# Listing all engines' order in the second network of a linear-attention and two-network kernel, with sums in place and its second layer bank by bank

## The chip, the core and the metric

The kernel runs on one core of a Trainium2 chip. The core has five engines that run their own instruction lists in order: TensorE (PE, matrix products into PSUM), VectorE (DVE), ScalarE (ACT), GpSimd (POOL) and SyncE (SP), which here issues nearly all DMAs. The metric is the time of one execution on the device in microseconds, as the median of several runs.

## What is computed

```python
def reference(q, k, v, alpha, moe_w_in, moe_w_out, domain_probs, w1, w2):
    for t in range(768):                               # linear attention, 4 batches, 8 heads, 48 wide
        state = alpha[:, :, t, :, None] * state + einsum('bhd,bhe->bhde', k[:, :, t], v[:, :, t])
        y[:, :, t] = einsum('bhd,bhde->bhe', q[:, :, t], state)
    x = tokens(y)                                      # 3072 x 384
    x = elu(x @ w_in) @ w_out                          # first network, hidden 2048
    p = domain_probs / (domain_probs.sum(-1, keepdims=True) + 1e-9)
    for e in range(4):                                 # second network, 4 experts, hidden 1024 each
        out += p[:, e:e + 1] * (relu(x @ w1[e]) @ w2[e])
    return out
```

## The kernel before

All large products keep float32 accuracy by splitting every operand into a high part in the TensorE format `fp32r` and a remainder: `hi` by a cast, `low = value - hi` by a subtraction. One 128x128 by 128x512 product then is three matmuls (hi·hi, hi·low, low·hi).

The attention and the first network fill the first 546 us. The change touches the second network, at the end of `run`. Its tokens are worked on in three *pairs* r of 1024 tokens (two chunks of 512); a pair has two halves m of 512 columns and three 128-row blocks of the model's width. The hidden units of all four experts are 32 blocks of 128, taken three at a time: a *group* i = 11 r + q is three hidden blocks (two for q = 10), so there are 33 groups.

*Layer 1* of a group (`layer1`, L699) needs the product of a 3x3 weight block by a 3x2 x block, 18 tile products; a bilinear scheme does it with 15 (`STEPS`, 11 for q = 10: `STEPS2`). Each of the 15 steps multiplies one precomputed sum of weights by one precomputed sum of x tiles (three matmuls, L717) into one of two PSUM banks `h0` and `h1` in turn, and DVE adds the bank into running sums `u` (L731 to L737). Two of the additions per group run on POOL, `u<-u` in step 7 and `c<-u` in step 8, and one on DVE has both its inputs in SBUF, `u<-u` in step 7. Six steps (5, 8, 10, 12, 13 and 14) finish a hidden tile (m, f): (1,2), (1,0), (1,1), (0,2), (0,1), (0,0). A finished tile lies in a buffer `c`; `relu` (L693) has ACT write its `hi` (L695) and the ReLU in place (L696), and POOL the remainder into `g` (L697). The `c` buffers come from `ctile` (L640), five in rotation, out of pools that others share: every fifth lies in the tag `g` of the pool `hp`, three buffers, where the `xh` tiles below live too.

*Layer 2* of group i-1 (`layer2`, L745) runs on PE between the steps of layer 1 of group i: the list `work` is cut by a count of DVE operations (`cut`) and a piece is issued after each step. A group with three hidden blocks has 54 matmuls (two halves, three output blocks d, three hidden blocks f, three matmuls each) into six PSUM banks `oa[m, d]`, named a0, a1, h2 for m = 1 and t0, t1, t2 for m = 0. When an expert's last hidden block is done in a bank, `gate` (L776) has DVE multiply the bank by the expert's probability into a `c` (for the first expert straight into `acc`) and POOL add it to `acc` (L787). So an ordinary group is 45 + 54 = 99 matmuls. Gates fall in q = 3, 6, 8 and in q = 0 of the next pair, where SP then stores `acc` to the output.

*The next pair's x.* The 15 sums of x tiles for pair r + 1 are made during pair r by `prep_x` (L607): a load of the raw x and 15 times `one`, which adds up tiles on POOL (L633), casts `hi` on ACT and writes the remainder on POOL (`split`, L370), into a tile `xh` that SP stores to DRAM (L636). `load_xc` brings them back as `xc` when the old ones are free. Groups q = 1 to 7 take up to three of these 16 jobs each, after steps 1, 6 and 11.

*What sets the order.* In the first network the instructions of PE, ACT, DVE and POOL stand as the program writes them (`tc.manual_schedule`), and `later` puts a function in a queue that the next `flush` runs, so that a dependent instruction is listed some work behind the one it waits for. In the second network only PE is listed by hand; a scheduler orders ACT, DVE, POOL and SP from its own estimate, and `later` runs its function at once. Nothing orders SP by hand in either.

Of the kernel before, what the change touches and what calls it, by code (L numbers as in the profile page):

```python
# [86 lines left out]
class _Fast:  # L87
# [605 lines left out]
    def relu(self, g, n, v):  # L693
# [3 lines left out]
        nc.gpsimd.tensor_tensor(out=g[:, n, 1], in0=v, in1=g[:, n, 0].bitcast(F32), op=ALU.subtract)  # L697

    def layer1(self, i, extra):  # L699
# [45 lines left out]
    def layer2(self, i, G):  # L745
# [14 lines left out]
        if i == NPR * NG - 1:  # L760
            runs = [[(t, d) for t in items if t[0] == m] for m in (1, 0) for d in range(KD)]
        for run in runs:
            for (m, f), d in run:
                e, n = divmod(hid(f), F2)
                for j, (wl, gl) in enumerate(((0, 0), (0, 1), (1, 0))):
                    def mm(m=m, f=f, d=d, wl=wl, gl=gl, e=e, first=n == 0 and j == 0, last=n == F2 - 1 and j == 2):
                        nc.tensor.matmul(  # L767
                            oa[m, d], wt[:, f, wl, d * 128:(d + 1) * 128], G[m][:, f, gl], start=first, stop=last
                        )
                        if last:  # L770
                            self.gate(r, e, m, d)

                    l.append(mm)
# [424 lines left out]
```

## Time and profile before

| what | value |
|---|---|
| median of 3 runs | 1299.26 us (1299.12 to 1302.6) |
| the profiled execution | 1300.14 us, its span 1298.3 us |
| PE busy | 1249.2 us, 96% of the span |
| DVE busy | 896.5 us, 69% |
| ACT busy | 585.6 us, 45% |
| POOL busy | 521.5 us, 40%, nearly all of it in the second network |
| chain that ended last | PE 78%, DVE 9%, ACT 4%, POOL 3% of the span |

Matmuls are pipelined, so a busy PE is not a PE at its best rate; the distance from one matmul's start to the next's is the better measure, and the length of a group is taken from it. A profile's time stamps belong to one execution, the one of 1300.14 us. A wait is put down to the semaphore that came last.

### The profile page before, as it was taken

How to read it: one execution, taken by the hardware profiler on the slowest of the kernel's cores; microseconds unless marked ns; L12 is line 12 of the kernel's file. 1: busy time of each engine (PE TensorE's matmuls, PEld its weight loads, DVE VectorE, ACT ScalarE, POOL GpSimd, SP SyncE). 2: the span in 40 equal slices, each digit the busy share in tenths (PEclk: the TensorE clock that was granted, in tenths of full speed). 3: DMA queues.
4: the chain of work that ended last, by engine and by line, in shares of the span. 5: the costliest groups of instructions: out<-in, count | busy, mean ns of one | idle time of the engine just before them, and what ended most of it. 6: DMA issues, size and time to landing. Idle time of an engine off the chain costs nothing.

```text
span 1298.3 us, 17667 instructions
## 1 busy us (share of the span) xinstructions
PE 1249.2 (96%) x6457; PEld 1013.5 (78%) x6457; DVE 896.5 (69%) x1510; ACT 585.6 (45%) x1076; POOL 521.5 (40%) x405
## 2 busy tenths in 40 slices
PE   8887899999999999899999999899999999999997
PEld 6665788888888788778878887788878878888886
DVE  8988677786777757666757666566767576657664
ACT  5665556666666666544342323334332233233241
POOL 0000000000000005478776656887956465456562
PEclk8998999999999999999999999999999999999999
DMA  6554156564756455727646458755644574425232
GB/s 226 201 177 141 62 182 219 189 207 170 250 189 211 167 189 206 275 91 255 231 175 230 150 191 319 266 204 203 249 166 169 206 293 172 176 103 206 98 114 72
DMA packets 71535, 246.70 MB, mean 190 GB/s; under 512 B 6680, under 2 KB 38264, under 8 KB 62096
## 3 DMA queue, kind: packets, MB, share of 16 engines
q1 hardware_dynamic: 70576, 240.77, 52.4%
q10 hardware_dynamic: 864, 4.72, 0.9%
q8 instruction: 53, 0.87, 0.3%
q14 instruction: 42, 0.34, 0.1%
HBM read 182.11 MB, written 63.36 MB: 189 GB/s over the span
## 4 chain that ended last, share of the span: by engine, by line
PE 78%; DVE 9%; ACT 4%; POOL 3%; issue 3%; DMA 1%; SPq 0%; POOLq 0%; ACTq 0%; DVEq 0%
PE h L717 22%; PE t L767 13%; PE h L417 12%; PE t L445 12%; PE a L767 9%; PE h L767 4%; DVE u L737 1%; PE a L247 1%; PE a L304 1%; PE a L311 1%; DVE w_W L373 1%; DVE cv L79 1%; DVE cv L82 1%; DMA xraw<-x1d 1%; POOL g_W L697 1%
## 5 line engine op out<-in xcount | busy, mean ns | idle before, releaser
L737 DVE TENSOR_TENSOR u<-h,u 128x512 f32<-128x512 f32 x258 | 177.6, 688 | 91.0 <-PE h L717 89.8
L417 PE MATMUL h<-x,w_W 128*128 128x512 f32 x864 | 219.8, 398 | 11.6 <-DVE w_W L373 7.0
L717 PE MATMUL h<-xc_Q,wa 128*128 128x512 f32 x780 | 220.2, 392 | 5.0 <-DVE c L737 2.4
L445 PE MATMUL t<-g,w_W 128*128 128x512 f32 x864 | 214.8, 392 | 3.5 <-DVE g L435 3.5
L697 POOL TENSOR_TENSOR g_W<-c,g_W 128x512 fp32r<-128x512 f32 x128 | 164.4, 1300 | 125.9 <-ACT c L696 108.0
L562 POOL TENSOR_TENSOR xs<-xr 128x512 f32<-128x512 f32 x8 | 11.1, 1405 | 482.0 <-DMA xr<-x1d 482.0
L695 ACT ACTIVATE g_W<-c 128x512 fp32r<-128x512 f32 x128 | 80.0, 626 | 276.5 <-DVE c L737 163.9
L417 PEld LDWEIGHTS h<-x,w_W 128*128 128x128 f32 x864 | 161.4, 190 | 50.4 <-DVE w_W L373 10.4
L445 PEld LDWEIGHTS t<-g,w_W 128*128 128x128 f32 x864 | 160.7, 188 | 38.6 <-DVE g L435 4.7
L717 PEld LDWEIGHTS h<-xc_Q,wa 128*128 128x128 f32 x780 | 146.2, 188 | 38.5 <-DVE u L737 4.4
L767 PE MATMUL t<-g_W,wb 128*128 128x512 f32 x576 | 157.6, 389 | 0.0
L767 PEld LDWEIGHTS t<-g_W,wb 128*128 128x128 f32 x576 | 108.1, 188 | 22.6 <-POOL g_W L697 0.2
L696 ACT ACTIVATE c<-c 128x512 f32<-128x512 f32 x192 | 121.0, 632 | 7.7 <-ACT g_W L695 0.4
L737 DVE TENSOR_TENSOR c<-u,h 128x512 f32<-128x512 f32 x123 | 84.1, 686 | 51.7 <-PE h L717 37.9
L428 DVE SCALAR_TENSOR_TENSOR h<-e,h 128x512 f32<-128x512 f32 x96 | 66.5, 693 | 74.0 <-ACT e L427 74.0
L717 PE MATMUL h<-xc_W,wa 128*128 128x512 f32 x390 | 110.9, 393 | 6.1 <-DVE u L737 4.1
L731 DVE COPY u<-h 128x512 f32<-128x512 f32 x99 | 68.1, 691 | 68.1 <-PE h L717 67.8
L767 PE MATMUL a<-g_W,wb 128*128 128x512 f32 x384 | 113.6, 395 | 0.7 <-POOL g_W L697 0.7
L697 POOL TENSOR_TENSOR g_X<-c,g_X 128x512 fp32r<-128x512 f32 x64 | 82.2, 1296 | 62.5 <-ACT c L696 51.9
L695 ACT ACTIVATE g_X<-c 128x512 fp32r<-128x512 f32 x64 | 40.0, 627 | 142.5 <-DVE c L737 78.4
L435 DVE TENSOR_TENSOR g<-h,g 128x512 fp32r<-128x512 f32 x96 | 65.9, 686 | 41.1 <-ACT g L433 40.7
L717 PEld LDWEIGHTS h<-xc_W,wa 128*128 128x128 f32 x390 | 73.2, 189 | 23.9 <-DVE u L737 5.5
(138 smaller groups left out, 1948.6 us busy)
## 6 DMA issues: line engine op xcount, KB each, us to landing
wa<-wad SPq DMA_DIRECT2D x33, 1536.0 KB, 6.5
wb<-wbd SPq DMA_DIRECT2D x30, 1536.0 KB, 7.2
raw<-in_att_dram SPq DMA_DIRECT2D x22, 960.0 KB, 4.9
wad<-wh SPq DMA_DIRECT2D x44, 384.0 KB, 2.7
wbd<-wh SPq DMA_DIRECT2D x43, 384.0 KB, 3.5
xcd<-xh SPq DMA_DIRECT2D x30, 512.0 KB, 3.0
wraw<-in_wm_dram SPq DMA_DIRECT2D x16, 768.0 KB, 4.2
wraw<-in_we_dram SPq DMA_DIRECT2D x20, 576.0 KB, 4.5
```

The lines of the kernel that those rows point to most:

```text
L79: nc.vector.scalar_tensor_tensor(out=t, in0=top, scalar=-0x80000000, in1=t, op0=ALU.bitwise_and, op1=ALU.bitwise_or)
L417: nc.tensor.matmul(h[:, 0:n], w[:, wl, fi, k * 128:(k + 1) * 128], x[:, xl, k, n0:n0 + n], start=(k == 0 and i == 0), stop=(k == KD - 1 an ...
L428: nc.vector.scalar_tensor_tensor(out=h, in0=e, scalar=-1.0, in1=h, op0=ALU.add, op1=ALU.max)
L435: 0, lambda: nc.vector.tensor_tensor(out=g[:, 1], in0=h, in1=g[:, 0].bitcast(F32), op=ALU.subtract)
L445: nc.tensor.matmul(self.xa[k][:, 0:n], w[:, wl, fi, DM + k * 128:DM + (k + 1) * 128], g[:, gl, 0:n], start=(first and i == 0), stop=(last ...
L695: nc.scalar.activation(out=g[:, n, 0], in_=v, func=AF.Relu)
L696: nc.scalar.activation(out=v, in_=v, func=AF.Relu)
L697: nc.gpsimd.tensor_tensor(out=g[:, n, 1], in0=v, in1=g[:, n, 0].bitcast(F32), op=ALU.subtract)
L717: nc.tensor.matmul(b, w[:, wl], x[:, xl], start=(j == 0), stop=(j == 2))
L731: nc.vector.tensor_copy(out, b)
L737: (nc.vector if "b" in (a0, a1) or dst == "S5" else nc.gpsimd).tensor_tensor(out=out, in0=val(a0, b), in1=val(a1, b), op=ALU.add if op == ...
L767: nc.tensor.matmul(oa[m, d], wt[:, f, wl, d * 128:(d + 1) * 128], G[m][:, f, gl], start=first, stop=last)
```

## The change

1. The listed order of PE, ACT, DVE and POOL is kept on through the second network, and so is the queue: `layer1` flushes it at the start of each step. The remainder of a ReLU (`relu`) and the addition of a gate (`gate`) are put in the queue once, so they stand behind the next flush. `later` gets a count n, by which a function waits n flushes.
2. `one` adds its tiles up in the place of the remainder, `t[:, 1]`, and takes no `c`; the cast is listed two flushes later, remainder and store three. Two jobs per group, after steps 2 and 9, in q = 1 to 8. The load of the first `xc` tile moves from step 0 to step 4 of q = 9.
3. `layer2` sorts its products by expert, half, output block d, hidden block f, where before it was expert, half, f, d. The last group already stood bank by bank.

```diff
-    def later(self, f):
+    def later(self, f, n=1):
         if self.queue is None:
             f()
+        elif n > 1:
+            self.queue.append(lambda: self.later(f, n - 1))
         else:
             self.queue.append(f)
...
-            t = self.hp.tile([128, 2, 512], F32R, tag="g", name="xh")
+            t = self.hp.tile([128, 2, 512], F32, tag="g", name="xh")
             l = terms(p)
             v = x[l[0][0]]
-            if len(l) > 1:
-                c = self.ctile()
-                for u, sign in l[1:]:
-                    nc.gpsimd.tensor_tensor(out=c, in0=v, in1=x[u], op=ALU.add if sign > 0 else ALU.subtract)
-                    v = c
-            self.split(t[:, 0], t[:, 1], v, nc.gpsimd)
-            nc.sync.dma_start(out=self.xcd[r - 1][n // 3][:, n % 3], in_=t.bitcast(F32))
+            for u, sign in l[1:]:
+                nc.gpsimd.tensor_tensor(out=t[:, 1], in0=v, in1=x[u], op=ALU.add if sign > 0 else ALU.subtract)
+                v = t[:, 1]
+            hi = t[:, 0].bitcast(F32R)
+
+            def low():
+                nc.gpsimd.tensor_tensor(out=t[:, 1].bitcast(F32R), in0=v, in1=t[:, 0], op=ALU.subtract)
+                nc.sync.dma_start(out=self.xcd[r - 1][n // 3][:, n % 3], in_=t)
+
+            self.later(lambda: nc.scalar.copy(hi, v), 2)
+            self.later(low, 3)
...
-        nc.gpsimd.tensor_tensor(out=g[:, n, 1], in0=v, in1=g[:, n, 0].bitcast(F32), op=ALU.subtract)
+        self.later(
+            lambda: nc.gpsimd.tensor_tensor(out=g[:, n, 1], in0=v, in1=g[:, n, 0].bitcast(F32), op=ALU.subtract)
+        )
...
+            self.flush()
             b = self.hbank()
...
-        runs = [[(t, d)] for t in items for d in range(KD)]
+        items = sorted(((hid(f) // F2, -m, d, f) for m, f in items for d in range(KD)))
...
+        if r < NPR - 1 or e < NE - 1:
+            self.later(lambda: add(nc.gpsimd))
+        else:
+            add(nc.vector)
...
-        self.queue = None
-        order.__exit__(None, None, None)
...
-                if 1 <= q <= 7:
-                    for n, s in enumerate(xs[(q - 1) * 3:q * 3]):
-                        put(1 + 5 * n, do, s)
+                if 1 <= q <= 8:
+                    for n, s in enumerate(xs[(q - 1) * 2:q * 2]):
+                        put(2 + 7 * n, do, s)
```

Three places show what this does to the engines' lists. First POOL in group 12 (pair 1, q = 1), where the raw x of the next pair arrives. `g<-c,g` is a remainder, `u<-u` and `c<-u` are layer 1's two additions, `c<-xraw` and then `xh<-xraw` a sum. Before:

```order
L697 TENSOR_TENSOR g_W_7555<-c,g_W_7555 128x512
L737 TENSOR_TENSOR u<-u 128x512
L737 TENSOR_TENSOR c<-u 128x512
L633 TENSOR_TENSOR c<-xraw 128x512 x2
L697 TENSOR_TENSOR g_W_7555<-c,g_W_7555 128x512
L633 TENSOR_TENSOR c<-c,xraw 128x512 x2
L697 TENSOR_TENSOR g_W_7555<-c,g_W_7555 128x512
L373 TENSOR_TENSOR xh<-c,xh 128x512 x2
```

And POOL in the same group now:

```order
L704 TENSOR_TENSOR g_W_7541<-c,g_W_7541 128x512
L746 TENSOR_TENSOR u<-u 128x512
L746 TENSOR_TENSOR c<-u 128x512
L704 TENSOR_TENSOR g_W_7541<-c,g_W_7541 128x512
L633 TENSOR_TENSOR xh<-xraw 128x512
L633 TENSOR_TENSOR xh<-xh,xraw 128x512 x2
L704 TENSOR_TENSOR g_W_7541<-c,g_W_7541 128x512
L638 TENSOR_TENSOR xh<-xh 128x512
```

The sums of one product instead of two stand there, behind the remainder of tile (1,0) and ahead of that of (1,1), and they write no `c`.

Second, DVE in group 8 (pair 0, q = 8) from step 5 to step 10, where `c<-a,pb`, `c<-h,pb` and `c<-t,pb` are gates of the six banks and the others are layer 1. Before:

```order
L737 TENSOR_TENSOR c<-h_6843,u 128x512
L786 TENSOR_TENSOR c<-a_5441,pb 128x512
L737 TENSOR_TENSOR u<-h_6860,u 128x512
L786 TENSOR_TENSOR c<-a_5442,pb 128x512
L737 TENSOR_TENSOR u<-h_6871,u 128x512
L786 TENSOR_TENSOR c<-h_5443,pb 128x512
L737 TENSOR_TENSOR u<-u 128x512
L737 TENSOR_TENSOR u<-h_6886,u 128x512
L733 SCALAR_TENSOR_TENSOR u<-h_6899,u 128x512
L737 TENSOR_TENSOR c<-u,h_6907 128x512
```

And DVE over the same steps now:

```order
L746 TENSOR_TENSOR c<-h_6827,u 128x512
L792 TENSOR_TENSOR c<-a_5438,pb 128x512
L746 TENSOR_TENSOR u<-h_6844,u 128x512
L746 TENSOR_TENSOR u<-h_6852,u 128x512
L746 TENSOR_TENSOR u<-u 128x512
L792 TENSOR_TENSOR c<-h_5439,pb 128x512
L746 TENSOR_TENSOR u<-h_6867,u 128x512
L742 SCALAR_TENSOR_TENSOR u<-h_6880,u 128x512
L746 TENSOR_TENSOR c<-u,h_6890 128x512
L792 TENSOR_TENSOR c<-t_5434,pb 128x512
```

One gate now stands at step 2 (ahead of these rows), one at step 5, one after `u<-u` of step 7, and the next at step 10.

Third, PE at the start of a group without gates (group 2: pair 0, q = 2), where L717 is layer 1 and L767 layer 2 of the group before, banks a, a, h of the half m = 1. Before:

```order
L717 MATMUL h_5646<-xc_Q_4865,wa 128x512 x3
L767 MATMUL a_5441<-g_W_5511,wb 128x512 x2
L717 MATMUL h_5658<-xc_Q_4865,wa 128x512 x3
L767 MATMUL a_5441<-g_W_5511,wb 128x512
L767 MATMUL a_5442<-g_W_5511,wb 128x512 x3
L717 MATMUL h_5675<-xc_Q_4865,wa 128x512 x3
L767 MATMUL h_5443<-g_W_5511,wb 128x512 x3
L767 MATMUL a_5441<-g_W_5511,wb 128x512
```

And PE at the same place now:

```order
L726 MATMUL h_5636<-xc_Q_4865,wa 128x512 x3
L773 MATMUL a_5437<-g_W_5508,wb 128x512 x2
L726 MATMUL h_5648<-xc_Q_4865,wa 128x512 x3
L773 MATMUL a_5437<-g_W_5508,wb 128x512 x4
L726 MATMUL h_5659<-xc_Q_4865,wa 128x512 x3
L773 MATMUL a_5437<-g_W_5508,wb 128x512 x3
L773 MATMUL a_5438<-g_W_5508,wb 128x512
```

The first nine matmuls of layer 2 now go to one bank and read all three hidden tiles of the half; before, they read the first tile alone, three matmuls to each bank.

## Rows read from the trace of the kernel before

**Rows 1.** The page: engines' busy time; and one costly group, with its mean duration

```profile
PE 1249.2 (96%) x6457; PEld 1013.5 (78%) x6457; DVE 896.5 (69%) x1510; ACT 585.6 (45%) x1076; POOL 521.5 (40%) x405
...
L695 ACT ACTIVATE g_W<-c 128x512 fp32r<-128x512 f32 x128 | 80.0, 626 | 276.5 <-DVE c L737 163.9
```

**Rows 2.** PE's waits, 560 us to the end: total us, times, longest us

```profile
PE h L717 <- DVE u L737: 6.4, 7, 3.9
PE h L717 <- DVE c L737: 4.3, 4, 2.2
PE a L767 <- POOL g_W L697: 0.7, 1, 0.7
PE h L717 <- DVE ok L802: 0.4, 1, 0.4
```

**Rows 3.** Groups 1, 5, 7, 8, 11, 12, 13, 17, 23: start:end, length, PE, PEld, DVE, ACT, POOL, clock

```profile
563.27:588.22 24.95, 24.60 (x102) 19.84 (x103) 13.50 (x21) 7.98 (x14) 20.25 (x17) 0.93 0.16 62
655.54:679.46 23.92, 23.01 (x101) 18.51 (x100) 14.04 (x21) 11.58 (x20) 17.20 (x14) 1.00 0.49 180
701.92:724.36 22.44, 22.44 (x101) 18.58 (x100) 13.45 (x20) 7.41 (x13) 10.74 (x9) 1.00 0.38 140
724.36:747.31 22.95, 22.75 (x101) 18.50 (x99) 16.54 (x25) 7.22 (x13) 13.93 (x11) 1.00 0.42 150
789.47:808.54 19.07, 18.80 (x83) 15.05 (x82) 14.96 (x23) 5.04 (x10) 12.04 (x10) 1.00 0.87 340
808.54:836.62 28.08, 23.18 (x101) 18.25 (x99) 14.63 (x22) 9.78 (x18) 22.21 (x19) 1.00 0.70 249
836.62:860.85 24.23, 24.23 (x100) 19.83 (x100) 14.14 (x21) 10.34 (x19) 22.90 (x18) 0.93 0.63 237
928.17:952.31 24.14, 22.74 (x101) 18.50 (x99) 19.29 (x26) 7.97 (x14) 20.30 (x17) 1.00 0.73 286
1058.89:1082.84 23.95, 22.98 (x100) 18.43 (x99) 15.11 (x23) 9.77 (x18) 17.44 (x15) 1.00 0.64 226
836.60:841.60 5.00, 4.99 (x15) 3.94 (x16) 2.67 (x4) 2.27 (x5) 5.00 (x5) 0.66 0.91 320
```

**Rows 4.** PE in order of time: start us, us, instruction [idle before, releaser]

```profile
701.92 0.84 PE L717 MATMUL h<-xc_Q,wa 128*128 128x512 f32 x3
...
810.81 0.96 PE L717 MATMUL h<-xc_W,wa 128*128 128x512 f32 x3 [0.98 <-DVE c L737]
```

**Rows 5.** SP, POOL, ACT and DVE in order of time, group 12

```profile
817.25 4.24 SPq L555 DMA_DIRECT2D xraw<-x1d  x4
...
827.64 2.54 POOL L633 TENSOR_TENSOR c<-xraw 128x512 f32<-128x512 f32 x2 [2.65 <-DMA xraw<-x1d]
...
834.05 1.14 ACT L372 CAST xh<-c 128x512 fp32r<-128x512 f32 x2 [6.49 <-POOL c L633]
...
835.27 0.69 DVE L737 TENSOR_TENSOR c<-u,h 128x512 f32<-128x512 f32 x1 [5.78 <-POOL g_W L697]
```

**Rows 6.** ACT and DVE in order of time, groups 4 and 5

```profile
641.98 0.62 ACT L372 CAST xh<-c 128x512 fp32r<-128x512 f32 x1 [7.12 <-DMA xcd<-xh]
...
657.28 0.69 DVE L737 TENSOR_TENSOR c<-u,h 128x512 f32<-128x512 f32 x1 [3.14 <-POOL g_W L697]
```

**Rows 7.** POOL's groups by line, second network: busy us, mean ns, idle before

```profile
L697 POOL TENSOR_TENSOR g_W<-c,g_W 128x512 fp32r<-128x512 f32 x126 | 161.9, 1300 | 125.7 <-ACT c L696 107.8 <-issue 17.0 <-POOL acc L787 0.8
...
L787 POOL TENSOR_TENSOR acc<-acc,c 128x512 f32<-128x512 f32 x48 | 62.4, 1320 | 33.3 <-DVE c L786 33.3
L737 POOL TENSOR_TENSOR u<-u 128x512 f32<-128x512 f32 x32 | 52.8, 1650 | 7.4 <-DVE u L737 7.3
```

**Rows 8.** DVE in order of time: `u<-u` in groups 8 and 17

```profile
737.14 1.42 DVE L737 TENSOR_TENSOR u<-u 128x512 f32<-128x512 f32 x1
...
939.97 3.61 DVE L737 TENSOR_TENSOR u<-u 128x512 f32<-128x512 f32 x1
```

**Rows 9.** The flag's tile: operation, count, duration ns min/median/max, first and last start

```profile
L797 DVE TENSOR_REDUCE flag_r<-pacc x1: 205/205/205, 439.6 to 439.6; 128x1 f32<-128x48 f32 x1
```

More of the change, by code (lines that the diff above doesn't have):

```diff
@@ L751, in layer2 @@
         items = [(m, f) for m in range(2) for f in range(3) if q < NG - 1 or f != 1]
-        items.sort(key=lambda t: (hid(t[1]) // F2, -t[0], t[1]))
         l = []
@@ L758, in layer2, with mm @@
         oa = self.oa[r]
-        runs = [[(t, d)] for t in items for d in range(KD)]
[L760 to L773, printed above, removed]
+        items = sorted(((hid(f) // F2, -m, d, f) for m, f in items for d in range(KD)))
+        for e, m, d, f in items:
+            m, n = -m, hid(f) % F2
+            for j, (wl, gl) in enumerate(((0, 0), (0, 1), (1, 0))):
+                def mm(m=m, f=f, d=d, wl=wl, gl=gl, e=e, first=n == 0 and j == 0, last=n == F2 - 1 and j == 2):
+                    nc.tensor.matmul(
+                        oa[m, d], wt[:, f, wl, d * 128:(d + 1) * 128], G[m][:, f, gl], start=first, stop=last
+                    )
+                    if last:
+                        self.gate(r, e, m, d)
+                l.append(mm)
         return l
@@ L786, in gate, with add @@
         nc.vector.tensor_tensor(out=t, in0=bank, in1=pb, op=ALU.mult)
-        (nc.gpsimd if r < NPR - 1 or e < NE - 1 else nc.vector).tensor_tensor(out=acc, in0=acc, in1=t, op=ALU.add)
-        if e == NE - 1:
-            nc.sync.dma_start(
-                out=self.out[d, :, 2 * r:2 * r + 2, m * 256:(m + 1) * 256],
-                in_=acc.rearrange("p (c t) -> p c t", c=2),
-            )
+        def add(eng):
+            eng.tensor_tensor(out=acc, in0=acc, in1=t, op=ALU.add)
+            if e == NE - 1:
+                nc.sync.dma_start(
+                    out=self.out[d, :, 2 * r:2 * r + 2, m * 256:(m + 1) * 256],
+                    in_=acc.rearrange("p (c t) -> p c t", c=2),
+                )
+        if r < NPR - 1 or e < NE - 1:
+            self.later(lambda: add(nc.gpsimd))
+        else:
+            add(nc.vector)
     def flag(self):
@@ L955, in run @@
             self.flush()
-        self.queue = None
-        order.__exit__(None, None, None)
         assert not slots and not post and not loads
-        pe_order = tc.manual_schedule(engines={mybir.EngineType.PE})
-        pe_order.__enter__()
         ng = NPR * NG
@@ L974, in run @@
             if i == ng:
+                while self.queue:
+                    self.flush()
                 for f in work:
@@ L991, in run @@
                     xs = self.prep_x(r + 1)
-                if 1 <= q <= 7:
-                    for n, s in enumerate(xs[(q - 1) * 3:q * 3]):
-                        put(1 + 5 * n, do, s)
+                if 1 <= q <= 8:
+                    for n, s in enumerate(xs[(q - 1) * 2:q * 2]):
+                        put(2 + 7 * n, do, s)
                 if q == NG - 2:
-                    put(0, self.load_xc, r + 1, 0)
+                    put(4, self.load_xc, r + 1, 0)
                 if q == NG - 1:
@@ L1016, in run @@
             assert not plan
-        pe_order.__exit__(None, None, None)
+        order.__exit__(None, None, None)
         self.p2m.__exit__(None, None, None)
```

## The prediction

> **What bounds the kernel now.** I read the page first, then PE's waits, then stretches one group long, then the engines behind each wait. PE is busy 96% of the span [rows 1]. The change leaves the attention and the first network as they are on every compute engine, so only the second network counts, from 546 us on. All that PE waits for there is 11.8 us: 7 waits for DVE's `u`, the longest 3.9, 4 for DVE's `c`, one for POOL's `g`, one of 0.4 for the flag [rows 2]. The reader should see how narrow that makes the question: no matmul is removed, so the change can only take back these waits and what follows them, or add new ones.
>
> I measure in groups. Group 7 takes 22.44 us for 99 matmuls, 0.2267 us each [rows 3], and that is the length of every 99-matmul group in which nothing waits. Three places are much longer: group 5 by 1.48, groups 12 and 13 by 5.64 and 1.79, group 17 by 1.70 [rows 3]. The loss of group 13 is no wait: after the stop of 3.9 us the granted clock is 0.66 over its first 5 us [rows 3], between the levels of 1.2 and 2.4 GHz. Group 1 loses 2.51 (it begins behind group 0, where no layer 2 stretches PE's time and DVE bounds), group 23 1.51, groups 11 and 22 0.71 each (19.07 for 81 matmuls), groups 8, 19 and 30 0.5 each; 1, 8, 11 and 23 stand for them in [rows 3]. That is some 17.5 us in all.
>
> **Why they wait.** Group 12: the next pair's raw x is issued at 817.25, and POOL stands 2.65 us until it lands at 827.64 [rows 5]. POOL's list has the sums ahead of the remainders of L697, and ACT stands 6.49 us before the casts of those sums, with two more tiles' ReLUs behind them. So DVE waits 5.78 us before 835.27 for a `c` buffer that POOL has not finished reading [rows 5], and PE waits for DVE. The sums themselves take buffers out of that rotation of five. Group 5 is the same chain from another cause: ACT idles 7.12 us before a cast, until an older `xh` is stored out of the same three buffers, and DVE in the end waits 3.14 us for POOL [rows 6]. Group 17: DVE's one operation with both inputs in SBUF (`u<-u`) takes 3.61 us while POOL runs without a gap [rows 8].
>
> **The change, part by part.** POOL's own work in a group, six remainders at 1.30, `u<-u` at 1.65 [rows 7] and `c<-u`, is 10.7 us, as group 7 shows [rows 3]. Sums and remainders for the next pair are 17 + 15 = 32 instructions per pair before and after, 1.3 us each. Before, they stand three steps to a group in five groups and one in a sixth; now two in eight, behind steps 2 and 9, 3 to 5 instructions or 4 to 6.5 us a group. A gate's six additions are 7.9 us (1.32 each) [rows 7]. So POOL has 16 us of 22.44 in an ordinary group, 22.6 in groups 6 and 17, and 23.9 in 8 and 19, where the new eighth share falls.
>
> *Sums in place, listed order (groups 5, 12, 13).* `c` buffers go only to ReLUs and gates now; a cast stands two steps behind its sums, the remainder three. I walk group 12 by hand. The ReLU of step n reaches POOL 0.84 (three matmuls [rows 4]), 0.69 (DVE) and 1.25 us (two ACT operations of 0.63 [rows 1]) after step n starts: 2.8 us. Group 11 leaves POOL some 9 us behind; the output stores wait for that, and the raw x comes behind them on SP, so it lands at 828.5 or so, not earlier than now. Three sums of one product take POOL to 832.4, the remainder of tile (1,1) ends at 833.7, the last one by 839. But DVE's ReLU of step 13 needs the buffer of group 11's last gate, that of step 14 one of step 5: both long free. So the stop goes, and the 1.79 of clock in group 13 with it. What stays is the stop at 810.81, 0.98 us [rows 4], with what follows some 1.4: in the short group 11 (81 × 0.2267 = 18.4 us of PE) POOL has 18.7 us of work and DVE 18.2. Group 12 gives 5.6 - 1.4 = 4.2, group 13 1.8. Group 5: an `xh` now comes back a whole group before it is wanted, and POOL ends 2.7 us into the next group, so 1.5.
>
> *Group 17.* By the same walk its six additions start 4 us into the group and POOL is not free before 16; DVE's `u<-u` is due at 11.7. In group 8 it gets in at the end of one POOL instruction, 1.42 us [rows 8], and PE loses little; in group 17 it loses its turn twice more. I take the 1.7 as given back, and a race of this kind elsewhere as a rival. The Trainium skill, page "SBUF — State Buffer", section "SBUF: two separate sides", says that the two engines share a port pair as an exclusive lock, held for a whole instruction, which goes to whoever starts first. By that page the wait would be one POOL instruction, 1.3 us by the rows, and the sum would stay; the 3.61 us is more than one instruction, so the row decides.
>
> *Bank by bank.* The matmuls of one half now go to a bank nine at a time. In groups 8, 19 and 30 gates fall in steps 2, 5, 7, 10, 13 and 14, not in 5, 6, 7, 13, 14, 14; three in a row come ahead of the stop there. But DVE's `u<-u` still meets the addition of step 5, and PE's step 10 still waits on what follows it: I count 0.3 us in all, between 0 and 2.9 (all of groups 8, 11, 19, 22 and 30), near the lower end since DVE is as full as before. In 6, 17 and 28 the gated part has one tile per bank and no order changes. The price is a deadline: the remainder of (1,1) is wanted by the fifth matmul of layer 2, 2.3 us into the next group, not by the eleventh, at 5 us. By the walk POOL has it 2.5 us ahead of the group's start in ordinary groups, 0.4 us after it in group 7, 1.4 after in group 13, a margin of 0.9: 0.
>
> *Flag.* A reduction of 0.205 [rows 9], a comparison and a memset of one column, done long ahead today, now stand in DVE's list between step 4's operations and PE's matmul on them. DVE has just come free there, so PE loses some 0.6 us (between 0.2, the reduction alone, and 1, all three with as much again for the waits between them). ACT's copies of the first network's last result move by a step; nobody near waits for them. On SP `wb` stands behind stores of `xh`, at most some 3 us into its group, and is wanted 17 us in; its cover is 7 us of landing, so 0. The tail's lists are the same.
>
> Sum: 1.5 + 4.2 + 1.8 + 1.7 + 0.3 - 0.6 = 8.9 us. The profiled execution took 1300.14 us (span 1298.3), 0.9 above the median of 1299.26; against it the sum gives 1291.2, against the median 1290.4.
>
> **Rivals.** *The listed order takes out nearly all waits*: the gate bursts too (2.6 more) and half of what starts groups 12 and 23 (1.5): 13 us, 1286. For it: the gates are apart and POOL has 6 us free in ordinary groups. Against: DVE and POOL stay full in groups 11 and 22.
>
> *The waits move.* Stores, raw x and sums keep their order, so part of group 12's stop stays; `u<-u` loses its turn in two or three of the eight gated groups, 1.7 each as in group 17; in 8 and 19 POOL's 23.9 us hold up DVE's last ReLUs, which have under 1 us to spare. Two such losses and half of groups 12 and 13 are 3.4 + 3: 8.9 - 6.4 = 2.5, so 1296 to 1297. It is also what comes if the change does little of what it says.
>
> *Slower: the deadline.* PE stops at the start of groups because the remainder of (1,1) is late. It decides at 2.3 us into a group. If POOL ran 4.8 us later than walked in ordinary groups (a cast that waits for sums, with ReLUs behind it in ACT's list, could do that), every further 0.8 us would cost the 16 groups with sums 13 us, more than the 8.9 gained: 1303. Against it: that lead of 2.5 us in ten of them, and POOL's 6 idle us.
>
> **How the numbers follow.** Forecast 0.55, its own range 1287.5 to 1293.5; nearly all waits 0.13; waits that move 0.21; slower 0.11. Measurements of this kernel can tell about 0.3%, 3.9 us, from no change, so faster is below 1295.4: the forecast, the first rival and 0.06 of the second make 0.74. The second's rest is 0.15 for the same, the third 0.11. The range runs from 1285.5, just past the first rival, to 1297, the end of the second; the deadline lies outside.
>
> **What would show it.** Group 12 some 23.8 us long without DVE's wait for `c` at its end, and group 13 at full clock; group 5 at 22.44; no ACT wait for a store of `xh`; PE's waits down from 11.8 us to some 5, most of it in group 1 and at the starts of 12 and 23; no DVE `u<-u` above 1.8 us; a flag stop of about 1 us in group 1. The forecast is wrong if layer 2 waits for POOL at the start of groups (the deadline), if a long `u<-u` is followed by a PE wait (the race), or if POOL gets the raw x only beyond 830 and DVE's `c` waits again (group 12).

## The result

| kernel | median us | lowest to highest, runs | second network's loss, us |
|---|---|---|---|
| before, beside after | 1299.19 | 1298.93 to 1302.60, 4 | 17.55 |
| after | 1289.05 | 1287.17 to 1290.16, 4 | 5.05 |

The ratio is 0.9914, with a 95% interval of 0.9893 to 0.9935; the prediction was 1290.4. The last column is read from one trace of each kernel, as in the prediction: the lengths of the groups 0 to 31, less what each has where nothing waits (22.44 us for 99 matmuls, 19.72 for 87, 18.36 for 81, and the 17.0 of group 0). It is the better gauge of small edits, with one caution: each loss is of one execution. In fourteen traces group 0 began between 543.30 and 548.91 us, though the lists up to there are all but the same, and that spread lies in every median; the losses leave it out. The profiled execution of after took 1288.27 us, 11.9 less than the 1300.14 of before: 12.5 in the groups, 0.5 of it lost again ahead of them.

The page of the kernel after, first the busy time that answers to [rows 1], then the shares of the chain that ended last:

```profile
PE 1246.8 (97%) x6453; PEld 1013.7 (79%) x6457; DVE 894.0 (69%) x1510; ACT 587.3 (46%) x1076; POOL 522.0 (41%) x405
...
PE 84%; DVE 7%; ACT 4%; issue 2%; POOL 1%; DMA 1%; DVEq 0%; ACTq 0%; POOLq 0%
```

No engine does more or less than before; PE stands less. Its waits from 540 us to the end in the kernel after (total us, times, longest us), against the 11.8 us of [rows 2]:

```profile
PE h L726 <- DVE c L746: 2.9, 3, 2.1
PE h L814 <- DVE flag_r L812: 0.8, 1, 0.8
PE h L726 <- DVE u L746: 0.7, 2, 0.4
PE a L773 <- POOL g_X L704: 0.2, 1, 0.2
```

These are 4.6 us in seven waits (from 560 us on, where [rows 2] begins, the same seven). The groups 1, 5, 8, 11, 12, 13, 17 and 23 of the kernel after, in the columns of [rows 3]:

```profile
563.75:587.54 23.79, 23.01 (x102) 18.70 (x103) 13.86 (x24) 8.31 (x15) 15.81 (x13) 1.00 0.23 85
654.86:677.29 22.43, 22.43 (x100) 18.58 (x99) 13.44 (x20) 9.47 (x17) 17.08 (x14) 1.00 0.52 193
722.17:744.88 22.71, 22.71 (x101) 18.50 (x100) 17.12 (x25) 9.26 (x16) 20.21 (x17) 1.00 0.39 137
787.03:806.05 19.02, 18.66 (x83) 15.12 (x81) 15.28 (x24) 5.67 (x10) 12.68 (x11) 1.00 0.78 311
806.05:829.44 23.39, 23.01 (x100) 18.43 (x99) 15.01 (x23) 6.67 (x11) 17.07 (x14) 1.00 0.86 294
829.44:851.90 22.46, 22.46 (x100) 18.51 (x99) 13.44 (x20) 11.53 (x20) 20.11 (x16) 1.00 0.61 224
919.22:941.66 22.44, 22.44 (x100) 18.58 (x99) 17.33 (x26) 6.70 (x12) 19.77 (x17) 1.00 0.63 209
1047.95:1071.07 23.12, 22.74 (x101) 18.50 (x99) 14.91 (x23) 9.25 (x16) 16.87 (x14) 1.00 0.74 261
```

Groups 5, 13 and 17 have no loss left, group 12 has 0.95 of its 5.64, and the clock of group 13 is full.

Group 12, where the raw x of the next pair arrives, in order of time on SP, PE, POOL, ACT and DVE of the kernel after, as [rows 5] had it:

```profile
816.30 3.71 SPq L557 DMA_DIRECT2D xraw<-x1d  x4
...
807.73 0.97 PE L726 MATMUL h<-xc_W,wa 128*128 128x512 f32 x3 [0.38 <-DVE c L746]
...
827.62 2.66 POOL L633 TENSOR_TENSOR xh<-xh,xraw 128x512 f32<-128x512 f32 x2 [0.88 <-DMA xraw<-x1d]
830.24 1.30 POOL L704 TENSOR_TENSOR g_W<-c,g_W 128x512 fp32r<-128x512 f32 x1
...
830.32 0.62 ACT L641 CAST xh<-xh 128x512 fp32r<-128x512 f32 x1 [5.85 <-POOL xh L633]
...
826.75 0.69 DVE L746 TENSOR_TENSOR c<-u,h 128x512 f32<-128x512 f32 x1 [0.36 <-POOL xh L633]
```

The raw x comes in two halves, and each trace has its own axis, so the times are best counted from the start of group 12, 806.05 here and 808.54 before. POOL waits for the second half until 827.62, 21.6 us into the group; the first sum, on the first half, started at 825.45, 19.4 us in. The row of [rows 5] at 827.64 is the first half, 19.1 us in. POOL is through with the three sums at 830.28 and with the remainder of (1,1) at 831.54, and ACT still stands 5.85 us before a cast. But the longest that DVE waits behind the sums for POOL is 0.36 us instead of 5.78. The data comes as late as before, and it no longer holds up a buffer that layer 1 needs.

### The profile page after: what moved, and what is told of

Read it like the earlier page. It is cut to its first block, busy times and chain, and to the rows that moved or that the text cites. A ratio compares the mean times of both kernels' runs of the same rounds, so it can differ in the third digit from the quotient of the medians.

```text
span 1286.4 us, 17672 instructions
## 1 busy us (share of the span) xinstructions
PE 1246.8 (97%) x6453; PEld 1013.7 (79%) x6457; DVE 894.0 (69%) x1510; ACT 587.3 (46%) x1076; POOL 522.0 (41%) x405
## 4 chain that ended last, share of the span: by engine, by line
PE 84%; DVE 7%; ACT 4%; issue 2%; POOL 1%; DMA 1%; DVEq 0%; ACTq 0%; POOLq 0%
PE h L726 24%; PE t L773 14%; PE t L447 13%; PE h L419 13%; PE a L773 10%; PE h L773 5%; PE a L249 2%; PE a L306 1%; PE a L313 1%; DVE w_W L375 1%; PE h L270 1%; DVE P L204 1%; DVE cv L79 1%; DVE wh L375 1%; ACT cv L405 1%
## 5 line engine op out<-in xcount | busy, mean ns | idle before, releaser
L447 PE MATMUL t<-g,w_W 128*128 128x512 f32 x864 | 218.1, 397 | 3.5 <-DVE g L437 3.5
L773 PE MATMUL a<-g_W,wb 128*128 128x512 f32 x384 | 108.2, 389 | 0.0
```

Source lines behind the costliest of these rows:

```text
L447: nc.tensor.matmul(self.xa[k][:, 0:n], w[:, wl, fi, DM + k * 128:DM + (k + 1) * 128], g[:, gl, 0:n], start=(first and i == 0), stop=(last ...
L773: nc.tensor.matmul(oa[m, d], wt[:, f, wl, d * 128:(d + 1) * 128], G[m][:, f, gl], start=first, stop=last)
```

## The experiments

Each trace is read as losses by group. The medians were taken at different times, each beside runs of the kernel before (medians of 1298.54 to 1300.11), so ratios compare better than medians. The table has the parts of the change, alone and in pairs, in us of the second network:

| groups | before | sums alone | banks alone | list alone | sums + banks | list + sums | all three (after) |
|---|---|---|---|---|---|---|---|
| 1 | 2.51 | 2.52 | 2.56 | 1.32 | 2.54 | 1.35 | 1.34 |
| 5, 6 | 1.50 | 0 | 1.57 | 8.19 | 0 | 0 | 0 |
| 8, 19, 30 | 1.48 | 1.47 | 0.52 | 0.64 | 2.43 | 0.91 | 0.80 |
| 9, 20 | 0 | 1.45 | 0 | 0 | 1.17 | 5.81 | 0 |
| 11, 22 | 1.42 | 1.41 | 1.38 | 1.37 | 1.49 | 1.31 | 1.26 |
| 12 | 5.64 | 1.49 | 4.35 | 5.94 | 1.27 | 2.16 | 0.95 |
| 13 | 1.79 | 0 | 2.89 | 5.50 | 0.79 | 0 | 0.02 |
| 17 | 1.70 | 0 | 0 | 4.09 | 0 | 0 | 0 |
| 23 | 1.51 | 1.27 | 1.27 | 2.13 | 1.25 | 1.95 | 0.68 |
| all 32 | 17.55 | 9.60 | 14.55 | 30.03 | 10.93 | 13.48 | 5.05 |

### One part at a time

**Sums alone**: the kernel before with part 2 (sums in place, two jobs a group, the first load of `xc` at step 4), everything else as it was.

```diff
-            self.flush()
             b = self.hbank()
...
-        items = sorted(((hid(f) // F2, -m, d, f) for m, f in items for d in range(KD)))
+        bank = i == NPR * NG - 1
+        items = [(hid(f) // F2, -m, d, f) for m, f in items for d in range(KD)]
+        items.sort(key=lambda t: (t[0], t[1], t[2], t[3]) if bank else (t[0], t[1], t[3], t[2]))
...
+        self.queue = None
+        order.__exit__(None, None, None)
...
+        order = tc.manual_schedule(engines={mybir.EngineType.PE})
+        order.__enter__()
```

(The diff is against the kernel after; what is not in it is part 2.)

> The kernel before with part 2 alone: sums in place, two jobs a group, the first load of xc at step 4; ACT, DVE and POOL in the scheduler's order, layer 2 tile by tile. It completes the table of the parts. If the parts added, bank by bank (3.3 alone) and the sums would make order_not_listed's 7.0, so 3.7 for this one: 1295, with groups 5 and 12 given back (1.5 and some 4) and group 17 a draw. The rival, that the sums pay only where the gates are spread by the bank order: groups 12 or 13 keep over 2 us, a start after gates waits for a c, 1297 to 1299.

Measured: 1292.75 us (4 runs) against 1300.11, ratio 0.9934 [0.9913, 0.9955], about twice the gain I expected. Its groups 12 and 17, in the columns of [rows 3]:

```profile
807.92:831.85 23.93, 22.99 (x101) 18.43 (x99) 15.32 (x23) 7.80 (x14) 18.35 (x16) 1.00 0.65 226
...
921.61:944.05 22.44, 22.44 (x101) 18.58 (x99) 17.32 (x26) 6.24 (x11) 19.32 (x16) 1.00 0.60 208
```

Groups 5 and 13 come out at 22.44 like 17, and group 12 at 23.93, all with the scheduler's order. So what the prediction called "sums in place, listed order" is part 2 alone; the list is not needed for it. Which of its pieces does it without the list, the sums in place, the two jobs a group or the later load, was not run; the runs under "Within part 2" take the first two apart with the list in place.

**Banks alone**: the kernel before with layer 2 bank by bank.

```diff
-        runs = [[(t, d)] for t in items for d in range(KD)]
-        if i == NPR * NG - 1:
-            runs = [[(t, d) for t in items if t[0] == m] for m in (1, 0) for d in range(KD)]
+        order = sorted((hid(f) // F2, -m, d, f) for m, f in items for d in range(KD))
+        runs = [[((-m, f), d) for e, m, d, f in order]]
```

> The kernel before, with layer 2 bank by bank and nothing else. If banks matter little: group 8 and its like 0.2 us shorter, groups 5, 12, 13 and 17 still long, 1298 to 1299. If the bank order is the cause: 1293 or less. The long u<-u of group 17 (3.61 us) is a race; that it is absent here with the same additions on POOL would say that any small shift ends it.

Measured: 1295.50 us (10 runs, 1289.64 to 1299.44) against 1298.77, ratio 0.9967 [0.9949, 0.9985]. That lies between the two cases that I had set. By the trace 3.0 us: 1.0 in the groups 8, 19 and 30, where the spread gates do what they should, and 1.7 in group 17, where `u<-u` took 1.11 us instead of 3.61. The gated part has one tile per bank there and PE's list did not change, so I take this for the draw of `u<-u`; one trace of each does not show it.

**List alone**: the listed order and the queue, with sums in a `c`, three jobs a group and layer 2 tile by tile. The cast stands right behind its sums again. The diff, against the kernel after, shows that and the spread of the jobs:

```diff
...
-            self.later(lambda: nc.scalar.copy(hi, v), 2)
-            self.later(low, 3)
...
+            self.split(t[:, 0], t[:, 1], v, nc.gpsimd)
...
-                if 1 <= q <= 8:
-                    for n, s in enumerate(xs[(q - 1) * 2:q * 2]):
-                        put(2 + 7 * n, do, s)
+                if 1 <= q <= 7:
+                    for n, s in enumerate(xs[(q - 1) * 3:q * 3]):
+                        put(1 + 5 * n, do, s)
...
```

> The changed list and queue alone: sums go to a c buffer, three jobs a group behind steps 1, 6 and 11 in seven groups, cast listed right behind its sums, layer 2 tile by tile. If the list is what counts: 1289 to 1291. If buffers and spreading count, DVE waits for c several us in groups 12 and 13 and perhaps in 2 to 5: 1295 to 1300, or slower than before, since three jobs now stand rigidly in POOL's and ACT's lists.

Measured: 1313.64 us (4 runs) against 1298.77, ratio 1.0106 [1.0082, 1.013]: slower, by 12.5 us of loss. First PE's waits in layer 2 of this kernel, then ACT, POOL and PE where groups 12 and 13 meet:

```profile
PE t L771 <- ACT g_W L697: 4.2, 2, 2.1
PE t L771 <- POOL g_W L700: 1.7, 2, 1.0
PE a L771 <- POOL g_W L700: 1.1, 1, 1.1
```

```profile
840.68 0.62 ACT L374 CAST xh<-c 128x512 fp32r<-128x512 f32 x1 [12.11 <-POOL c L635]
845.13 0.63 ACT L697 ACTIVATE g_W<-c 128x512 fp32r<-128x512 f32 x1 [3.83 <-POOL c L742]
...
841.38 1.26 POOL L375 TENSOR_TENSOR xh<-c,xh 128x512 fp32r<-128x512 f32 x1 [0.73 <-ACT xh L374]
842.60 1.27 POOL L742 TENSOR_TENSOR u<-u 128x512 f32<-128x512 f32 x1
...
844.65 1.65 PE L722 MATMUL h<-xc_W,wa 128*128 128x512 f32 x3 [3.63 <-DVE u L742]
```

ACT stands 12.11 us before the cast of a late sum, with ReLUs behind it; POOL's two additions of layer 1 stand behind the sums and the remainder of that product, and PE waits. The 1.65 us of that step, against 0.84 in [rows 4], is the granted clock again, 0.50 over those two microseconds. And layer 2 waits 7.0 us for `g`: the deadline, the prediction's slower rival, by the mechanism named there (a cast that waits for sums, ReLUs behind it). The largest single loss, 8.19 us in group 6, is 2.84 of these waits, a clock of 0.89 in the mean of the group, and a stop of 1.24 for a `u<-u` that took 3.45 us.

### Two parts

**Sums and banks** without the list: the kernel after with only PE listed in the second network.

```diff
-            self.flush()
             b = self.hbank()
...
+        self.queue = None
+        order.__exit__(None, None, None)
...
+        order = tc.manual_schedule(engines={mybir.EngineType.PE})
+        order.__enter__()
```

> The changed kernel, but in the second network only PE is listed and ACT, DVE and POOL are left to the scheduler; sums in place, two jobs a group and banks as changed. If the buffers and the spreading of the jobs are what counts, group 5 stays at 22.4 and group 12 below 24: 1289 to 1291. If the list is what counts, DVE waits for c in group 12 again and ACT for sums: 1294 to 1298.

Measured: 1291.82 us (4 runs) against 1298.77, ratio 0.9939 [0.9915, 0.9963]. Most of the gain is here without the list, and no more of it than with the sums alone (0.9934). Group 8 shows a lost turn of `u<-u` on DVE, 2.10 us of loss in that group:

```profile
736.04 3.34 DVE L745 TENSOR_TENSOR u<-u 128x512 f32<-128x512 f32 x1
```

**List and sums**, layer 2 tile by tile: the kernel after without part 3.

```diff
-        items = sorted(((hid(f) // F2, -m, d, f) for m, f in items for d in range(KD)))
+        bank = i == NPR * NG - 1
+        items = [(hid(f) // F2, -m, d, f) for m, f in items for d in range(KD)]
+        items.sort(key=lambda t: (t[0], t[1], t[2], t[3]) if bank else (t[0], t[1], t[3], t[2]))
```

> The changed kernel, with layer 2 put back to tile by tile (expert, half, hidden block, output block). If the banks matter little, as the prediction says, only groups 8, 19 and 30 grow from 22.7 to 22.9 or 23.0, some 0.7 us in all, and groups 5, 12, 13 and 17 stay as in the changed kernel: 1289 to 1290. If the bank order is what took the waits out, 4 us or more come back: 1293 or more.

Measured: 1296.08 us (10 runs) against 1298.77, ratio 0.9981 [0.9961, 1.0001]. The bank order, given the other two, is worth some 7 us in the medians and 8.4 in the traces, where I expected 0.7. Some 1.6 of the 8.4 are the granted clock, which fell behind the stop of 1.80 us in group 20 and did not behind the one of 1.75 in group 9. The loss is not in the gated groups (8, 19 and 30 lose 0.91 instead of 0.80) but at the start of the next ones, most of it in 9 and 20. DVE and then PE at the start of group 20 in this kernel:

```profile
992.21 0.69 DVE L794 TENSOR_TENSOR c<-t,pb 128x512 f32<-128x512 f32 x1 [1.03 <-PE h L726]
994.70 0.69 DVE L794 TENSOR_TENSOR c<-t,pb 128x512 f32<-128x512 f32 x1 [1.80 <-POOL g_W L704]
995.31 1.28 DVE L740 COPY u<-h 128x512 f32<-128x512 f32 x2
...
996.05 0.96 PE L726 MATMUL h<-xc_W,wa 128*128 128x512 f32 x3 [1.80 <-DVE u L740]
```

Its clock from 998 to 1000 us (columns of [rows 3]):

```profile
998.00:1000.00 2.00, 2.00 (x6) 1.55 (x5) 0.43 (x1) 0.00 (x0) 2.00 (x3) 0.50 1.12 473
```

And DVE at the same place of the kernel after:

```profile
986.39 0.69 DVE L746 TENSOR_TENSOR c<-u,h 128x512 f32<-128x512 f32 x1 [0.43 <-POOL g_W L704]
987.66 0.69 DVE L792 TENSOR_TENSOR c<-t,pb 128x512 f32<-128x512 f32 x1 [0.57 <-POOL acc L795]
988.26 1.28 DVE L740 COPY u<-h 128x512 f32<-128x512 f32 x2
```

Tile by tile, the last gates of half m = 0 fall so late that two are left for the start of the next group; each takes a `c`, and the second finds its buffer still read by a remainder on POOL. Layer 1's first copies stand behind it in DVE's list, so PE waits. Bank by bank one gate is left, and it waits 0.57.

### Within part 2

**Jobs by three**: the kernel after with the old spread of the 16 jobs (the `put` lines of list alone).

> The changed kernel, but three jobs a group behind steps 1, 6 and 11 in seven groups, as before. If spreading decides (xh buffers come back in time), ACT waits for stores of xh again and groups 2 to 5 and 13 to 16 lose 0.5 to 1.5 each: 1292 to 1298. If sums in place and the list are enough, groups 8 and 19 get lighter on POOL and nothing is lost: 1288 to 1290.

Measured: 1304.67 us (7 runs, 1297.82 to 1312.32) against 1298.54, ratio 1.0055 [1.0022, 1.0088]: slower than before, with 21.25 us of loss (3.62 of it in group 12, 4.99 in 13, 7.03 in 17), 16.2 more than after. The way was not the one I expected: ACT waits for no store of `xh`, and groups 2 to 5 and 14 to 16 lose nothing. DVE, POOL and PE in group 17 of this kernel:

```profile
937.99 5.99 DVE L746 TENSOR_TENSOR u<-u 128x512 f32<-128x512 f32 x1
...
937.20 2.55 POOL L795 TENSOR_TENSOR acc<-acc,c 128x512 f32<-128x512 f32 x2
939.70 1.30 POOL L704 TENSOR_TENSOR g_X<-c,g_X 128x512 fp32r<-128x512 f32 x1
940.94 1.27 POOL L795 TENSOR_TENSOR acc<-acc,c 128x512 f32<-128x512 f32 x1
942.16 1.27 POOL L746 TENSOR_TENSOR u<-u 128x512 f32<-128x512 f32 x1
...
944.63 1.65 PE L726 MATMUL h<-xc_Q,wa 128*128 128x512 f32 x3 [3.78 <-DVE u L746]
```

`u<-u` is issued at 937.99 and ends at 943.98, half a microsecond after the last of five POOL instructions without a gap. PE stops for 3.78 us, and the step after it takes 1.65 us. In group 17 of the kernel after, with two jobs, no `u<-u` takes over 1.6 us. The runs of this kernel spread over 14.5 us; that this is the same draw falling otherwise each time fits, but there is only the one trace, so it is not shown.

**Sums in a `c`**: the kernel after with the sums in a buffer of the rotation, as before.

```diff
+            c = self.ctile() if len(l) > 1 else None
             for u, sign in l[1:]:
-                nc.gpsimd.tensor_tensor(out=t[:, 1], in0=v, in1=x[u], op=ALU.add if sign > 0 else ALU.subtract)
-                v = t[:, 1]
+                nc.gpsimd.tensor_tensor(out=c, in0=v, in1=x[u], op=ALU.add if sign > 0 else ALU.subtract)
+                v = c
```

> The changed kernel, but the sums are made in a c buffer as before, not in place; order and places of the jobs as changed. A buffer taken by a sum comes back only with the remainder, three steps later and more. If c buffers decide: in groups 8 and 19, where gates take six of them too, DVE waits for c in the last steps, 2 to 4 us each, 1292 to 1297. If only the order decides: as the changed kernel, 1288 to 1290.

Measured: 1292.13 us (7 runs) against 1298.54, ratio 0.9943 [0.9922, 0.9964]; 2.7 us more loss than after, 2.42 of it in group 20, where a gate on DVE waits for the buffer of a sum (I had expected such waits in the groups 8 and 19 themselves):

```profile
990.24 0.69 DVE L793 TENSOR_TENSOR c<-t,pb 128x512 f32<-128x512 f32 x1 [3.48 <-POOL xh L639]
```

That a sum takes a buffer out of the rotation of five is so shown, but it is the smaller part of what part 2 brings.

### What was left

| groups | after | flag early | adds two flushes | adds three | pieces later | two edits together |
|---|---|---|---|---|---|---|
| 0, 1 | 1.34 | 0.92 | 1.35 | 2.96 | 1.69 | 0.94 |
| 8, 19, 30 | 0.80 | 0.78 | 0.80 | 0.28 | 0.84 | 0.81 |
| 9, 20 | 0 | 0 | 0 | 2.64 | 0 | 0 |
| 11, 22 | 1.26 | 1.28 | 1.27 | 2.31 | 1.30 | 1.27 |
| 12, 13 | 0.97 | 1.45 | 0 | 0.97 | 1.18 | 0 |
| 23 | 0.68 | 0.70 | 0 | 0.19 | 0.65 | 0 |
| all 32 | 5.05 | 5.13 | 3.42 | 9.35 | 5.67 | 3.02 |

**Flag early**: the reduction, comparison and memset listed ahead of the second network, in a function of their own.

```diff
+    def flag0(self):
+        r = self.flag_r = self.const.tile([128, 4], F32, name="flag_r")
+        nc.vector.tensor_reduce(out=r[:, 0:1], in_=self.pacc, axis=AX.X, op=ALU.add)
+        nc.vector.tensor_scalar(out=r[:, 2:3], in0=r[:, 0:1], scalar1=P_SUM, scalar2=None, op0=ALU.is_le)
+        nc.vector.memset(r[:, 3:4], 1.0)
...
+        at(b5 + 4, self.flag0)
```

> The changed kernel with the flag's reduction, comparison and memset listed in the first network again. If they cost what the trace shows (PE waits 0.8 us for them), group 1 goes from 23.8 to 22.9 or 23.0: 0.8 us less, 1288. If the time only moves to the next wait of a full DVE: no change.

Measured: 1289.57 us (4 runs) against 1298.54, ratio 0.9925 [0.9895, 0.9954], so nothing that the median shows. In the trace group 1 is 0.42 us shorter. PE around the flag, in the kernel after and then in this one:

```profile
572.10 0.19 PE L814 MATMUL h<-flag_r 128*1 128x1 f32 x2 [0.78 <-DVE flag_r L812]
```

```profile
572.71 0.19 PE L818 MATMUL h<-flag_r 128*1 128x1 f32 x2
573.25 0.96 PE L726 MATMUL h<-xc_Q,wa 128*128 128x512 f32 x3 [0.35 <-DVE ok L819]
```

The stop of 0.78 goes, and the wait behind it, 0.4 in [rows 2], comes back. Group 13 loses 0.50 in this trace, where the kernel after has 0.02. PE waits there for layer 2's `g`, the deadline of the prediction:

```profile
833.12 0.73 PE L773 MATMUL a<-g_W,wb 128*128 128x512 f32 x2 [0.21 <-POOL g_W L704]
```

**Additions two flushes late**: a gate's addition listed one step later than in the kernel after.

```diff
-            self.later(lambda: add(nc.gpsimd))
+            self.later(lambda: add(nc.gpsimd), 2)
```

> The changed kernel with a gate's addition on POOL listed two flushes after its product, not one, so that the addition of step 5 stands behind step 7's u<-u on POOL. If the meeting of DVE's u<-u with that addition is what makes PE lose 0.26 us in groups 8, 19 and 30: u<-u goes from 1.57 to 0.69 us there and the groups to 22.44, 0.8 us less. If DVE is simply full there, the groups stay at 22.7. Either way c buffers come back later, so the starts of groups 12 and 23 may lose up to 1 us more.

Measured: 1286.31 us (4 runs) against 1298.54, ratio 0.9911 [0.9877, 0.9946]. Groups 8, 19 and 30 stay as they were, so the first case of the expectation did not come; and groups 12 and 23, which were to lose up to 1 us more, lose nothing. POOL at the start of group 12, in the kernel after and in this one:

```profile
804.39 2.55 POOL L704 TENSOR_TENSOR g_X<-c,g_X 128x512 fp32r<-128x512 f32 x2 [1.41 <-ACT c L702]
```

```profile
801.49 1.29 POOL L795 TENSOR_TENSOR acc<-acc,c 128x512 f32<-128x512 f32 x1
802.93 2.57 POOL L704 TENSOR_TENSOR g_X<-c,g_X 128x512 fp32r<-128x512 f32 x2 [0.16 <-ACT c L702]
```

An addition now fills the 1.41 us in which POOL stood before two remainders, and POOL starts these two 1.25 us earlier against the start of the group (806.05 and 805.84); the `c` that DVE waits for there comes free that much sooner. In groups 8, 19 and 30 the addition of step 5 still stands directly ahead of layer 1's on POOL, and DVE's `u<-u` meets it, as in the kernel after.

**Additions three flushes late** (the same line with 3), to put that addition behind `u<-u`:

> The kernel after, with a gate's addition listed three flushes behind it. With two flushes groups 8, 19 and 30 kept their 0.26 us, as the addition of step 5's gate still stood ahead of layer 1's addition on POOL in step 7 and met DVE's u<-u (1.57 us). With three it stands behind: u<-u 0.7 us, groups 8, 19 and 30 at 22.44, groups 12 and 23 at 0 as with two flushes; in all 0.8 less than with two, 3.4 to 2.6 us of loss, 1285.5. The rival: additions that late hold the c buffers of the gates longer, DVE waits for a c in or behind the gated groups, and 1 us or more of loss is new.

Measured: 1292.81 us (4 runs) against 1300.11, ratio 0.9927 [0.9903, 0.9952]. Groups 19 and 30 lose nothing, as meant (8 keeps its 0.28), and 9, 20 and 22 lose more, 1.18, 1.46 and 1.03; another 1.6 is the clock in group 1. DVE in group 9 waits for the buffer that the late addition reads.

```profile
747.00 0.69 DVE L746 TENSOR_TENSOR c<-u,h 128x512 f32<-128x512 f32 x1 [1.98 <-POOL acc L795]
```

Of the three places, two is the best: three costs buffers, one leaves POOL's gap unfilled.

**Pieces later**: the first network's last two pieces in group 0 behind steps 5 and 9.

```diff
-                first_work = {1 + 3 * n: it for n, it in enumerate(items[-LA:])}
+                first_work = {5 + 4 * n: it for n, it in enumerate(items[-LA:])}
```

> The kernel after, with the first network's last two pieces in group 0 behind steps 5 and 9 instead of 1 and 4. Groups 0 and 1 are the largest loss that is left: group 0 takes 17.0 us for 63 matmuls of 0.2267 (14.28), group 1 loses 1.34. If the order at the start of group 0 is what makes DVE late, the two groups come out 1 to 2 us shorter in all, 1287 to 1288. The rival: DVE's work in group 0 bounds it wherever the pieces stand, or what they feed becomes late in group 1: groups 0 and 1 within 0.5 of after, 1289, or longer.

Measured: 1286.65 us (4 runs, 1284.94 to 1291.06) against 1300.11, ratio 0.9884 [0.986, 0.9908]. The median looks like a gain on the 1289.05, but the trace says otherwise: groups 0 and 1 lose 1.69 instead of 1.34, so the rival holds. The trace is of the slowest of the four runs, 1291.06, and its group 0 began last of all, at 548.91; that the other three were faster ahead of group 0 fits, and no trace shows it.

**The two edits together**: additions two flushes late and the flag early.

> The kernel after with the two edits that took loss away: a gate's addition two flushes later (the starts of groups 12 and 23) and the flag's three small operations listed ahead of the second network (group 1). The losses of the two should add, since they lie 480 us apart: group 1 0.92, groups 12 and 23 0, groups 8, 19 and 30 still 0.26, 11 and 22 still 0.65, 3.0 us in all where the kernel after has 5.05. The median some 2 us below the kernel after's 1289.05: 1287, and at or below the 1286.3 of the one edit. The rival: one of the starts of groups is a draw, as group 17 was before, and a loss of 1 to 2 us comes back in 12, 20 or 23: 1288 to 1290.

Measured: 1285.64 us (5 runs, 1285.05 to 1287.90) against 1298.83, ratio 0.9895 [0.9878, 0.9913]; 3.02 us of loss, as expected. It is the lowest loss of all. The median is some 3 us below that of the kernel after, but the intervals of the two ratios overlap, so the gain rests on the 2.0 us in the traces.

## Why the prediction was right, and where it was not

The sum was 8.9 us and the groups gave 12.5. The medians differ by 10.1, less than the 11.9 of the two traced executions; the spread ahead of group 0 is large enough for that. So that the forecast of 1290.4 lies within 1.4 us of the median is in part luck; its main mechanisms, in groups 5, 12 and 13, hold in the trace of after. Term by term:

- **Groups 5 and 13**: 1.48 and 1.77 against 1.5 and 1.8. No cast waits for a store any more.
- **Group 17**: 1.70 against 1.7. This was the long `u<-u` of [rows 8], which takes 1.54 us here. With the sums alone and with the banks alone the group loses nothing either. So the 1.7 may have been a draw in the one trace of before, and that it came back is not shown to be the change's doing.
- **Group 12**: 4.7 against 4.2. Counted from the start of the group, the walk had the raw x at 20.0 us and the remainder of (1,1) at 25.2; its halves came at 19.4 and 21.6 and the remainder at 25.5. What stays at the start of the group is 0.95 instead of 1.4.
- **Bank by bank**: 0.8 in the groups that I counted (0.7 in 8, 19 and 30, 0.16 in 11 and 22), against 0.3, inside the bounds. But these groups do not single out the bank order: list alone takes 0.84 from 8, 19 and 30, and undoing the banks gives back 0.11. The step behind the term was too narrow: I looked for the effect only in the gated groups and at the part by itself. With list and sums in place, undoing it costs 8.4 us, 7.0 of that in groups 9, 12 and 20 (1.6 of it the clock) and 1.3 in 23, because late gates then find no free `c` at the start of a group. The table does not add up by parts: 8.0 for the sums, 3.0 for the banks and -12.5 for the list would come to a loss of 1.5, where 12.5 were gained.
- **Flag**: 0.4 (a stop of 0.78 in place of the 0.4 of [rows 2]) against 0.6.
- **Group 23**, not in the sum: 0.8 gained.
- **Group 1**: a loss of 0.6 was forecast, a gain of 1.2 came. This is the clock, see below, and not shown to be the change. [rows 3] had a clock of 0.93 in this group before; the prediction read its loss as DVE's work in group 0 and overlooked that.

The 3.6 us beyond the sum are these: 0.5 in group 12, 0.5 in the groups counted for the bank order, 0.8 in group 23, 1.8 in group 1.

The attribution was wrong in one point. The terms of groups 5, 12 and 13 stood under "sums in place, listed order"; the sums give them without the list. What the list gives on top of sums and banks is 5.9 us by the traces, though alone it costs 12.5. But 1.2 of the 5.9 are in group 1, where the clock is in it, and 1.8 in group 8, the lost turn of one trace; 2.8 are left, in 20, 13, 23 and 12. The medians differ by 2.8 us and the intervals of the ratios overlap (0.9915 to 0.9963 and 0.9893 to 0.9935), so a gain from the list is likely and not clear of the noise.

Of the **rivals**, the deadline was real and near: list alone and jobs by three are its picture, with layer 2 waiting 7.0 and some 4 us for `g`. In the kernel after layer 2 waits 0.2 us once, at the very end. What kept it away is the spread of two jobs a group. The margin in group 13 is smaller than forecast, though: the remainder of (1,1) came 2.1 us into it where it is wanted at 2.3, not 1.4, since group 12 got shorter than walked. With the flag early it came too late, by 0.21 us. The lost turn of `u<-u` did not come in the trace of after, where the longest is 1.57 us:

```profile
733.98 1.57 DVE L746 TENSOR_TENSOR u<-u 128x512 f32<-128x512 f32 x1
...
733.72 1.29 POOL L795 TENSOR_TENSOR acc<-acc,c 128x512 f32<-128x512 f32 x1
```

POOL's addition was 0.26 us old when DVE issued `u<-u`, and DVE got in when it ended, unlike the 3.61 us of [rows 8]. It did come in three of the other traces: 3.34 us, 3.45 (list alone, group 6) and 5.99.

## What to carry to other kernels

Listing an order by hand is no gain in itself: here, with casts right behind their sums, it made the kernel 1% slower until the uneven work beside it (sums for later use, on the engine that others wait for) was spread to where that engine had gaps, and until the gates no longer came in a burst. Cost an edit in the company of the others, and look for its effect in the next group, where buffers of a shared rotation run out, and not only where its instructions move. Where medians spread by several microseconds for reasons that lie ahead of the changed part, compare the lengths of repeated stretches in the traces, which showed differences of 0.4 us. First set apart what changes by itself from one trace to the next: here a fall of the clock and a lost turn, each worth over 1 us.

## What the runs showed of the hardware

**The clock after a stop.** PE stops 2.15 us at the end of group 0 of the kernel after, and [rows 2] has 2.2 for the longest wait for `c` before. The granted clock fell behind it in all four kernels whose second network is not listed, and in one of ten that are. That one, additions three flushes late, has the same list as the kernel after up to there, and stopped 2.16 us before 565.57. Two microseconds each (columns of [rows 3]), first the kernel after, whose stop ended at 563.75, then this one:

```profile
564.00:566.00 2.00, 2.00 (x10) 1.60 (x10) 0.79 (x2) 1.94 (x5) 2.00 (x3) 1.00 0.32 135
566.00:568.00 2.00, 2.00 (x11) 1.64 (x10) 1.69 (x3) 1.57 (x3) 2.00 (x3) 1.00 0.00 0
```

```profile
566.00:568.00 2.00, 2.00 (x9) 1.60 (x8) 0.69 (x1) 1.94 (x4) 2.00 (x3) 0.77 0.25 104
568.00:570.00 2.00, 2.00 (x6) 1.57 (x5) 1.29 (x2) 1.41 (x3) 2.00 (x3) 0.50 0.00 0
```

The clock is 1.00, or it falls to 0.50, the level of 1.2 GHz, and the group is 1.6 us longer. So the same stop by the same list can cost 0 or 1.6 us more. Four of four unlisted kernels against one of ten listed makes a link with the list likely, but what it would be is open, and the 1.2 us that group 1 gained is not shown to be the change's. The Trainium skill, page "TensorE: Matmul & The Clock Gate", section "Part 1: The HAM clock gate (the "warmup" mystery)", calls the number of slow matmuls at a kernel's start variable from run to run; the two traces agree, and show it for a stop in the middle of a kernel.

**Lost turns.** DVE's operation with both inputs in SBUF took 3.34, 3.45, 3.61 and 5.99 us beside a POOL without gaps, and 0.69 where POOL was idle as it was issued (at 818.81 in the kernel after; POOL's own `u<-u`, which started 0.04 us behind it, took 1.80 instead of 1.3). The Trainium skill, page "SBUF — State Buffer", section "SBUF: two separate sides", lets whoever starts first have the shared ports for a whole instruction. The 1.57 us above agrees with a wait for one POOL instruction; 5.99 us does not, it is longer than four of 1.27 to 1.30. That DVE can lose several turns is measured; which rule gives the ports to POOL again was not tested.
